# Product 1 of the next block placed between products 5 and 3 in stages 2 and 4

## The chip, the cores and the metric

The kernel runs on one core of a Trainium2 chip. The metric is device time in microseconds (us), the median of repeated runs. Five instruction streams matter: TensorE (PE in the profile; its weight loads have a column of their own, PEld), VectorE (DVE), ScalarE (ACT), GpSimd (POOL) and SyncE (SP), whose queue issues all the transfers (DMA) between HBM and the on-chip memory.

## The reference

Three layers are chained. An attention with 32 memory slots per head is computed for 8 batches of 576 tokens and 8 heads of width 64:

```python
a = exp(phi - max(phi)); a = a / (sum(a) + 1e-9)
k_m, v_m = a^T k, a^T v                      # 32 x 64 per head
attn = softmax(q k_m^T / 8);  x = attn v_m   # 4608 x 512 after joining heads
```

Two feed-forward layers follow, on 4608 tokens with model width 512 and inner width 2048:

```python
h = x @ w_in;   g = s * relu(h)**2 + b;          x = g @ w_out
h = x @ w2_in;  g = h / (1 + exp(-1.702 * h));   y = g @ w2_out
```

## The kernel before, in words

All operands are float32. A product of two float32 matrices is made of three matmuls, since each operand is split into a high part (the cast to the matmul's format, `hi`, on ACT or DVE) and the rest (`lo`, a subtraction on DVE): high by high, high by low, low by high.

The work has four stages. Stage 1 makes, for every batch, the attention and the first inner product `h` with its `relu`, and sends the result `r` to HBM. Stage 2 (`down` with the name "wo") reads `r`, squares it on ACT and multiplies with `w_out`; stage 3 (`up`) makes the second inner product and its gate; stage 4 (`down` with the name "w2") makes the last product. Stages 2 to 4 go through 8 blocks of 576 tokens. In each block the product is made by Strassen's scheme in Winograd's form: seven products of half-size matrices instead of eight. They are numbered 1 to 7. In stages 2 and 4 each product runs over four quarters q of the inner dimension, and one quarter is a group of 12 matmuls of 288 columns (L611 to L613 of the profile): a product has 48 matmuls, a block 336, a stage 2688.

The seven products of a block go into three accumulators, tiles of PSUM: X (products 1, 6, 5 and 3, added one upon the other), Z (product 2) and Y (products 7 and 4). Since X goes on being added to, it has to be read out between products: after product 1 into `a`, after product 6 into `u2`, after product 5 into `u4`, after product 3 into the result `c12` (`leave`, L619; the copies are on ACT, L637 in stage 2 as two halves of 288 columns, L631 in stage 4 as one of 576). The group that adds to X next must wait for that copy. All accumulators, the `h` of stage 1 and some small products share one ring of 4 PSUM tiles ("ps" in `BUFS`, L179). The operands of the products, their quarters A, B, C, D, E and most results share a ring of 38 tiles ("t"), the weights a ring of 32 ("w"); of those, seven hold the kept quarter 3 of `w_out` and 21 more its other quarters throughout stage 2.

Nothing in this is put in order by hand. Every operation is given to `Order.add` with a due time, the engines that may do it, and what it reads and writes; `Order.sort` (L65) then plays the whole program with a cost for each operation and at each step takes, among the operations that could start soonest on an engine, those with the earliest due time. What comes out is the order of instructions on each engine, and each engine works through its own in order. A tile of a ring is given out in the order of due times too. In `down` the due time of quarter q of product i is `due + pos[i] * pas + q * step`, where `pas` is a seventh of a block (6.4) and `pos` (L576) the product's place. The loads of its operands are due 14 to 16 ahead of that (L583), their squares 5 ahead, the differences of quarters 4 ahead, the high and low parts 2.5 ahead.

Of the kernel before, what the change touches and what calls it, by code (L numbers as in the profile page):

```python
# [152 lines left out]
class Net:  # L153
# [415 lines left out]
    def down(self, name, src, s, due, prior, first):  # L569

        nc, T, HS = self.nc, self.T, self.HS
        pas = self.B2 / 7
        step = pas / 4
        X, Y, Z = (("ps", (x, name, s)) for x in "XYZ")
        G = [[("t", (x, name, s, q)) for x in "ABCDE"] for q in range(4)]
        pos = {1: 0, 2: 1, 6: 2, 7: 3, 5: 4, 3: 5, 4: 6}  # L576
        to = {1: X, 2: Z, 6: X, 7: Y, 5: X, 3: X, 4: Y}
        n = 2 * HS
        for x, i in zip((0, 2, 1, 3), (1, 2, 6, 6)):
            for q in range(4):  # L580
                d = due + pos[i] * pas + q * step
                k = G[q][x]
                self.load(d - 14 - 2 * (x == 1), k, src, s, q, x // 2, x % 2)  # L583
                if name == "wo":
                    self.on_act(d - 5, n, lambda k=k: nc.scalar.activation(T[k], T[k], AF.Square), (), (k,))
        for i, at in pos.items():
            for q in range(4):
                A, Bk, C, D, E = G[q]
                d = due + at * pas + q * step
                x = {1: A, 2: C, 6: E, 7: Bk, 5: A, 3: D, 4: C}[i]  # L590
                if i == 6:
                    self.minus(d - 4, A, Bk, A)
                    self.minus(d - 3.5, E, D, A, new=True)
                elif i == 7:
                    self.minus(d - 4, Bk, D, Bk)
                elif i == 4:
                    self.minus(d - 4, C, C, E)
                h, l = self.operand(d - 2.5, i, (name, s, q), x, n)
                w = ("w", (name, i, q) if (name, i, q) in self.kept else (name, i, q, 1))

                def mm(i=i, q=q, h=h, l=l, w=w):
                    z = to[i]
                    if q == 0 and i in (1, 2, 7):
                        self.pst(z)
                    for o in range(2):
                        out = T[z][:, o, 0:HS]
                        for p in range(2):
                            c = slice(256 * p + 128 * o, 256 * p + 128 * o + 128)
                            f = q == p == 0 and i in (1, 2, 7)
                            last = q == 3 and p == 1  # L610
                            nc.tensor.matmul(out, T[w][:, 0, c], T[h][:, p], start=f, stop=False, skip_group_check=True)  # L611
                            nc.tensor.matmul(out, T[w][:, 0, c], T[l][:, p], start=False, stop=False, skip_group_check=True)  # L612
                            nc.tensor.matmul(out, T[w][:, 1, c], T[h][:, p], start=False, stop=last, skip_group_check=True)  # L613

                self.pe(d, 12 * HS, mm, (h, l, (*w, "h"), (*w, "l")), (to[i],))
            d = due + (at + 1) * pas
            self.leave(name, s, i, to[i], d, X, Y, Z)
# [154 lines left out]
    def plan(self):  # L772
        B, B1, B2 = self.B, self.B1, self.B2
        t2 = B * B1
        self.order.until = t2
        t3, t4 = t2 + B * B2, t2 + 2 * B * B2
        self.kept = {("wo", i, 3) for i in range(1, 8)}
        self.warm(True)
        for i, x in enumerate(("moe_s", "moe_b")):
            self.dma(10, lambda i=i: self.sc[:, i:i + 1], lambda x=x: self.a[x].partition_broadcast(P), (), (("sc", 0, i),), 1)  # L780
        for b in range(B):
            s0 = b * B1
            if b == 0:
                for g in range(2):
                    self.slots(0, g, -42 + 4 * g, 10)
                    self.attend(0, g, -28 + 4 * g)
                self.warm(False)
            for j in range(4):
                if b == 0:
                    for c in range(4):  # L790
                        k = ("w", ("wi", j, c // 2))

                        def make(k=k, c=c):
                            if c % 2 == 0:
                                self.t(k, [P, 2, 512])
                            return self.T[k][:, c % 2]

                        self.convert(9.6 * j - 24 + 2 * c, (*k, c % 2), make, self.a["wi"][4 * j + c], 24 - 2 * c if j == 0 else 6)
                d = s0 + j * B1 / 4
                self.matrix(b, j, d - 8)  # L800
                for i in range(2):
                    for u in range(2):
                        self.step(b, 2 * j + i, u, d + B1 / 16 * (2 * i + u))
                if b + 1 < B and j < 2:
                    self.slots(b + 1, j, s0 + 2 + 8 * j)
                elif b + 1 < B:
                    self.attend(b + 1, j - 2, s0 + 18 + 7 * (j - 2))
            if b in (2, 3, 4, 6):
                q = (2, 3, 4, 6).index(b)
                self.prepare("wo", q, s0 + 2, keep=q == 3, step=3)  # L810
        for q in range(3):
            for i in range(1, 8):
                self.weights("wo", i, q, t2 - 12 + 6.2 * (1, 2, 6, 7, 5, 3, 4).index(i) + q * 1.5)
        for s in range(B):
            self.down("wo", "r", s, t2 + s * B2, None, s == 0)
        for q in range(4):
            self.prepare("w1", q, t2 + 10 + 115 * q, step=4)
        for q in range(4):
            for at, i in enumerate((1, 2, 6, 7, 5, 3, 4)):
                self.weights("w1", i, q, t3 - 14 + 11 * q + 1.5 * at)  # L820
        for s in range(B):
            self.up(s, t3 + s * B2)
        for q in range(4):
            self.prepare("w2", q, t3 + 10 + 65 * q, step=4)
        for at, i in enumerate((1, 2, 6, 7, 5, 3, 4)):
            for q in range(4):
                self.weights("w2", i, q, t4 - 14 + 6.2 * at + 1.5 * q)
        for s in range(B):
            self.down("w2", "g", s, t4 + s * B2, None, s == 0)
# [76 lines left out]
```

## Time and profile before

| | |
|---|---|
| median of 3 runs | 1437.73 us (1436.1 to 1439.28) |
| profiled execution, its own time | 1438.46 us |
| its span, first to last instruction | 1436.4 us |
| PE matmuls busy | 1400.5 us, 98% of the span |
| DVE, ACT busy | 1098.2 us (76%), 762.4 us (53%) |
| DMA | 329.19 MB, mean 229 GB/s |

The profile is one execution, and the span is 2.06 us shorter than the time of that execution. A matmul is shown with a length of about 0.29 us, while the next one starts about 0.13 us after it, because they are pipelined; so an idle time that the profile shows in front of a matmul is shorter than what the stream of matmuls loses there.

### The profile page before, as it was taken

What the parts mean: (1) busy time and instruction counts of PE and PEld (TensorE: products, weight loads), DVE (VectorE), ACT (ScalarE), POOL (GpSimd) and SP (SyncE); (2) the same over time, 40 slices, a digit from 0 to 9 for tenths busy, and PEclk for the clock granted to TensorE, in tenths of its full rate; (3) what the DMA queues carried; (4) which work ended last, traced back from release to release, by engine and by line L of the source; (5) the groups of instructions that cost most, each with busy time, mean ns of one, the idle gap of its engine ahead of it and who ended that gap; (6) DMA issues with size and microseconds to landing.
All of it is one profiled execution on the core that took longest, in us unless ns stands there. A gap on an engine that the chain in (4) does not pass through costs nothing.

```text
span 1436.4 us, 28622 instructions
## 1 busy us (share of the span) xinstructions
PE 1400.5 (98%) x11190; PEld 1340.0 (93%) x11190; DVE 1098.2 (76%) x1728; ACT 762.4 (53%) x1224; POOL 94.7 (7%) x70
## 2 busy tenths in 40 slices
PE   6899999999999999999999999999999999999998
PEld 5778877789999999999999999999999999999998
DVE  7879998986898988898895565752458787777872
ACT  4455654566676666665565555554444434243441
POOL 1400110100101000100110010100000000000000
PEclk9899999999999999999999999999999999999999
DMA  9979999899954465475998756473598433554330
GB/s 354 322 258 340 353 322 344 289 309 366 313 181 131 140 238 149 156 256 171 346 347 318 278 180 239 169 266 133 188 357 310 127 116 108 156 157 131 114 104 34
DMA packets 136775, 329.19 MB, mean 229 GB/s; under 512 B 15552, under 2 KB 15552, under 8 KB 136640
## 3 DMA queue, kind: packets, MB, share of 16 engines
q1 hardware_dynamic: 136640, 327.37, 66.2%
q8 instruction: 88, 1.44, 0.4%
q14 instruction: 47, 0.39, 0.1%
HBM read 192.56 MB, written 134.74 MB: 228 GB/s over the span
## 4 chain that ended last, share of the span: by engine, by line
PE 50%; DMA 1%; DVE 0%; issue 0%; ACT 0%; SPq 0%; DVEq 0%
PE X L611 5%; PE X L613 5%; PE X L612 5%; PE X L718 5%; PE X L720 5%; PE X L719 5%; PE Y L611 3%; PE Y L613 3%; PE Y L612 3%; PE Y L718 2%; PE Y L720 2%; PE Y L719 2%; PE Z L611 1%; PE Z L613 1%; PE Z L612 1%; PE Z L718 1%
## 5 line engine op out<-in xcount | busy, mean ns | idle before, releaser
L263 PE MATMUL h<-ah,mh 128*128 128x288 f32 x512 | 160.5, 313 | 4.7 <-DVE ah L242 4.5
L265 PE MATMUL h<-ah,ml 128*128 128x288 f32 x512 | 154.3, 301 | 9.3 <-DVE ml L247 9.1
L611 PE MATMUL X<-oh,wo 128*128 128x288 f32 x512 | 152.7, 298 | 9.8 <-ACT u L637 9.7
L264 PE MATMUL h<-al,mh 128*128 128x288 f32 x512 | 154.2, 301 | 2.1 <-DVE al L247 2.1
L611 PE MATMUL X<-oh,w 128*128 128x288 f32 x512 | 151.7, 296 | 0.7 <-ACT u L631 0.7
L718 PE MATMUL X<-oh,w 128*128 128x288 f32 x512 | 151.7, 296 | 0.2 <-DMA w<-w 0.2
L612 PE MATMUL X<-ol,wo 128*128 128x288 f32 x512 | 151.6, 296 | 0.0
L719 PE MATMUL X<-ol,w 128*128 128x288 f32 x512 | 151.1, 295 | 0.3 <-DVE ol L247 0.3
L612 PE MATMUL X<-ol,w 128*128 128x288 f32 x512 | 151.0, 295 | 0.0
L613 PE MATMUL X<-oh,wo 128*128 128x288 f32 x512 | 151.0, 295 | 0.0
L720 PE MATMUL X<-oh,w 128*128 128x288 f32 x512 | 150.5, 294 | 0.0
L613 PE MATMUL X<-oh,w 128*128 128x288 f32 x512 | 150.5, 294 | 0.0
L247 DVE TENSOR_TENSOR h<-Y,u 128x576 f32<-128x576 f32 x64 | 48.4, 757 | 128.7 <-ACT u L726 89.5
L547 ACT ACTIVATE r<-h 128x576 f32<-128x576 f32 x122 | 79.5, 651 | 110.2 <-PE h L265 90.8
L263 PEld LDWEIGHTS h<-ah,mh 128*128 128x128 f32 x512 | 99.8, 195 | 26.7 <-ACT r L547 12.0
L247 DVE TENSOR_TENSOR ol<-C,oh 128x576 fp32r<-128x576 f32 x128 | 94.9, 753 | 21.5 <-ACT oh L241 11.4
L265 PEld LDWEIGHTS h<-ah,ml 128*128 128x128 f32 x512 | 99.2, 194 | 10.5 <-DVE ml L247 10.5
L241 ACT CAST oh<-A 128x576 fp32r<-128x576 f32 x106 | 68.1, 672 | 74.3 <-PE Y L613 29.8
L611 PEld LDWEIGHTS X<-oh,wo 128*128 128x128 f32 x512 | 96.2, 188 | 11.7 <-ACT u L637 11.7
L247 DVE TENSOR_TENSOR ol<-A,oh 128x576 fp32r<-128x576 f32 x128 | 94.7, 760 | 15.3 <-PE X L613 5.7
L264 PEld LDWEIGHTS h<-al,mh 128*128 128x128 f32 x512 | 99.2, 194 | 2.9 <-DVE al L247 2.9
L746 ACT ACTIVATE g<-h 128x576 f32<-128x576 f32 x96 | 65.8, 686 | 67.5 <-DVE h L247 64.4
(181 smaller groups left out, 4226.8 us busy)
## 6 DMA issues: line engine op xcount, KB each, us to landing
w<-w SPq DMA_DIRECT2D x112, 512.0 KB, 5.7
r<-r SPq DMA_DIRECT2D x128, 288.0 KB, 4.1
g<-g SPq DMA_DIRECT2D x128, 288.0 KB, 2.7
wo<-wo SPq DMA_DIRECT2D x42, 512.0 KB, 5.2
kv<-in_kv SPq DMA_DIRECT2D x64, 258.0 KB, 4.8
raw<-in_w SPq DMA_DIRECT2D x32, 512.0 KB, 6.1
q<-in_q SPq DMA_DIRECT2D x32, 288.0 KB, 4.9
A<-r SPq DMA_DIRECT2D x32, 288.0 KB, 3.2
```

The lines of the kernel that those rows point to most:

```text
L241: self.order.add(due, [self.act(n, lambda: nc.scalar.copy(out(), src()), psum), self.dve(n, lambda: nc.vector.tensor_copy(out(), src()), f ...
L247: self.order.add(due, [self.dve(n, lambda: nc.vector.tensor_tensor(out(), a(), b(), op=op), port=port)], r, w, first)
L263: self.nc.tensor.matmul(ps, wh, xh, start=start and i == 0, stop=False)
L264: self.nc.tensor.matmul(ps, wh, xl, start=False, stop=False)
L265: self.nc.tensor.matmul(ps, wl, xh, start=False, stop=(i == n - 1))
L547: self.act(2 * HS, lambda: nc.scalar.activation(self.two(r), T[h][:, :, 0:HS], AF.Relu), psum=True),
L611: nc.tensor.matmul(out, T[w][:, 0, c], T[h][:, p], start=f, stop=False, skip_group_check=True)
L612: nc.tensor.matmul(out, T[w][:, 0, c], T[l][:, p], start=False, stop=False, skip_group_check=True)
L613: nc.tensor.matmul(out, T[w][:, 1, c], T[h][:, p], start=False, stop=last, skip_group_check=True)
L718: nc.tensor.matmul(out, T[w][:, 0, c], T[h][:, k], start=f, stop=False, skip_group_check=True)
L719: nc.tensor.matmul(out, T[w][:, 0, c], T[l][:, k], start=False, stop=False, skip_group_check=True)
L720: nc.tensor.matmul(out, T[w][:, 1, c], T[h][:, k], start=False, stop=k == 1, skip_group_check=True)
```

## The change

`pos` gives product 1 the place -3 instead of 0 and moves products 2, 6, 7 and 5 forward by one place each; 3 and 4 stay. Three places before a block begins is place 4 of the block before it, which is left empty there: the due times of product 1 of the next block fall between those of products 5 and 3. Since the loads, squares and parts of product 1 take their due times from it, they move with it, and so does the copy `a`. For the first block of stage 2 product 1 becomes due while stage 1 is still at work. The loads of `w_out` for stage 2 are due 12 earlier (and 6.4 instead of 6.2 apart); those of stage 4 are not touched. An empty line shifts the lines below by one, so L611 to L613 are L612 to L614 after the change.

```diff
--- before.py
+++ after.py
@@ -573,7 +573,8 @@
         step = pas / 4
         X, Y, Z = (("ps", (x, name, s)) for x in "XYZ")
         G = [[("t", (x, name, s, q)) for x in "ABCDE"] for q in range(4)]
-        pos = {1: 0, 2: 1, 6: 2, 7: 3, 5: 4, 3: 5, 4: 6}
+
+        pos = {1: -3, 2: 0, 6: 1, 7: 2, 5: 3, 3: 5, 4: 6}
         to = {1: X, 2: Z, 6: X, 7: Y, 5: X, 3: X, 4: Y}
         n = 2 * HS
         for x, i in zip((0, 2, 1, 3), (1, 2, 6, 6)):
@@ -810,7 +811,7 @@
                 self.prepare("wo", q, s0 + 2, keep=q == 3, step=3)
         for q in range(3):
             for i in range(1, 8):
-                self.weights("wo", i, q, t2 - 12 + 6.2 * (1, 2, 6, 7, 5, 3, 4).index(i) + q * 1.5)
+                self.weights("wo", i, q, t2 - 24 + 6.4 * (1, 2, 6, 7, 5, 3, 4).index(i) + q * 1.5)
         for s in range(B):
             self.down("wo", "r", s, t2 + s * B2, None, s == 0)
         for q in range(4):
```

The order that comes out differs on all engines from the end of stage 1 on. Two places on TensorE follow. The names are tiles with the number of their allocation; X is the accumulator, oh and ol are the high and low parts of an operand, wo is a tile of weights.

The first place is the end of product 5 and the start of product 3 of block 5 (the sixth) in stage 2. Before, on TensorE:

```order
L611 MATMUL X_1330_7345<-oh_1382_7720,wo_739_3886 128x288
L612 MATMUL X_1330_7345<-ol_1397_7821,wo_739_3886 128x288
L613 MATMUL X_1330_7345<-oh_1382_7720,wo_739_3886 128x288
L611 MATMUL X_1330_7345<-oh_1385_7739,wo_901_4781 128x288
L612 MATMUL X_1330_7345<-ol_1401_7843,wo_901_4781 128x288
L613 MATMUL X_1330_7345<-oh_1385_7739,wo_901_4781 128x288
```

Product 3 follows upon product 5 with nothing in between, both on the accumulator X of the same block. After, on TensorE at the same place:

```order
L614 MATMUL X_1328_7350<-oh_1387_7744,wo_740_3888 128x288
L612 MATMUL X_1408_7884<-oh_1394_7785,wo_736_3867 128x288
...
L614 MATMUL X_1408_7884<-oh_1394_7785,wo_736_3867 128x288
L612 MATMUL X_1408_7884<-oh_1397_7804,wo_658_3468 128x288
...
L614 MATMUL X_1408_7884<-oh_1397_7804,wo_658_3468 128x288
L612 MATMUL X_1328_7350<-oh_1400_7825,wo_882_4655 128x288
```

Two groups of 12 matmuls, quarters 2 and 3 of product 1 of the next block, which go into another X, now stand between the last group of product 5 and the first of product 3.

The same count for every seam in stage 2 at which X is read out before it is added to again: before, no group stands between products 5 and 3 in blocks 0, 2 and 5, nor between products 6 and 5 in blocks 2 and 6; one stands between 5 and 3 in blocks 1 and 7 (and between 1 and 6 in blocks 0 and 1), and two or more at all others. After, one group stands between 5 and 3 in block 7, which has no next block, and two or more at every other seam. In stage 4 one group or more stands there both before and after, except between 5 and 3 of block 7, where none does in either.

The second place is the end of stage 1. Before, on TensorE, the last `h` of stage 1 and the first product of stage 2:

```order
L263 MATMUL h_869_4593<-ah_800_4216,mh_849_4483 128x288
L264 MATMUL h_869_4593<-al_801_4218,mh_849_4483 128x288
L265 MATMUL h_869_4593<-ah_800_4216,ml_853_4505 128x288
L611 MATMUL X_873_4614<-oh_802_4220,wo_723_3815 128x288
L612 MATMUL X_873_4614<-ol_809_4244,wo_723_3815 128x288
L613 MATMUL X_873_4614<-oh_802_4220,wo_723_3815 128x288
```

Stage 2 begins when the last group of stage 1 is through. After, on TensorE:

```order
L614 MATMUL X_847_4456<-oh_781_4104,wo_736_3867 128x288
L263 MATMUL h_866_4558<-ah_782_4106,mh_836_4390 128x288
...
L265 MATMUL h_866_4558<-ah_804_4224,ml_838_4407 128x288
L612 MATMUL X_847_4456<-oh_785_4121,wo_658_3468 128x288
...
L614 MATMUL X_847_4456<-oh_785_4121,wo_658_3468 128x288
L263 MATMUL h_872_4597<-ah_782_4106,mh_836_4390 128x288
```

The quarters of product 1 of block 0 (X) now stand between groups of `h`: seven groups of `h` come while this X holds one of the four PSUM tiles.

## Rows read from the trace of the kernel before

**Rows 1.** The page, busy time of each engine.
```profile
PE 1400.5 (98%) x11190; PEld 1340.0 (93%) x11190; DVE 1098.2 (76%) x1728; ACT 762.4 (53%) x1224; POOL 94.7 (7%) x70
```
**Rows 2.** Busy time by stretch, stages 2 to 4; PEclk and DMA follow POOL.
```profile
345.00:710.00 365.00, 354.82 (x2634) 352.53 (x2633) 315.42 (x481) 245.13 (x413) 25.42 (x14) 1.00 0.64 213
710.00:1070.00 360.00, 359.83 (x2699) 359.60 (x2698) 211.54 (x335) 187.33 (x297) 25.47 (x18) 1.00 0.68 247
1070.00:1437.00 367.00, 361.64 (x2711) 361.17 (x2709) 275.97 (x402) 139.96 (x219) 0.00 (x0) 1.00 0.44 139
```
**Rows 3.** What PE waited for: us in total, times, longest us.
```profile
PE X L611 <- ACT u L637: 9.7, 6, 2.6
PE X L611 <- ACT u L631: 0.7, 1, 0.7
PE X L718 <- DMA w<-w: 0.2, 1, 0.2
```
**Rows 4.** Timeline of PE at seams with no group between: start, us, idle before.
```profile
373.56 0.29 PE L613 MATMUL X<-oh,wo 128*128 128x288 f32 x1
375.01 0.40 PE L611 MATMUL X<-oh,wo 128*128 128x288 f32 x1 [1.17 <-ACT u L637]
...
460.74 0.40 PE L611 MATMUL X<-oh,wo 128*128 128x288 f32 x1 [1.74 <-ACT u L637]
...
472.00 0.40 PE L611 MATMUL X<-oh,wo 128*128 128x288 f32 x1 [1.39 <-ACT u L637]
...
606.05 0.40 PE L611 MATMUL X<-oh,wo 128*128 128x288 f32 x1 [2.60 <-ACT u L637]
...
648.24 0.40 PE L611 MATMUL X<-oh,wo 128*128 128x288 f32 x1 [2.02 <-ACT u L637]
```
**Rows 5.** Timeline of PE at other seams, the last in stage 4.
```profile
366.86 0.29 PE L613 MATMUL Y<-oh,wo 128*128 128x288 f32 x1
367.19 0.40 PE L611 MATMUL X<-oh,wo 128*128 128x288 f32 x1
...
421.58 0.29 PE L613 MATMUL X<-oh,wo 128*128 128x288 f32 x1
421.94 0.40 PE L611 MATMUL X<-oh,wo 128*128 128x288 f32 x1
...
705.91 0.40 PE L611 MATMUL X<-oh,wo 128*128 128x288 f32 x1 [0.83 <-ACT u L637]
...
1419.31 0.40 PE L611 MATMUL X<-oh,w 128*128 128x288 f32 x1 [0.73 <-ACT u L631]
```
**Rows 6.** Timeline of ACT ahead of the stall that ends at 606.05.
```profile
603.21 0.68 ACT L585 ACTIVATE B<-B 128x576 f32<-128x576 f32 x1 [1.90 <-DMA B<-r]
603.80 0.66 ACT L241 CAST oh<-A 128x576 fp32r<-128x576 f32 x1
604.36 0.68 ACT L585 ACTIVATE C<-C 128x576 f32<-128x576 f32 x1
604.95 1.05 ACT L637 ACTIVATE u<-X,bw,sc 128x288 f32<-128x288 f32 x2
```
**Rows 7.** What SP's queue and ACT waited for in most of stage 2.
```profile
SPq L236 <- PE X L613: 57.8, 43, 4.4
...
ACT D L585 <- DMA D<-r: 7.3, 8, 2.5
```
**Rows 8.** The page, the evacuation of h in stage 1.
```profile
L547 ACT ACTIVATE r<-h 128x576 f32<-128x576 f32 x122 | 79.5, 651 | 110.2 <-PE h L265 90.8
```
**Rows 9.** The chain of waits: start, us, what; end of stage 2, start of stage 3.
```profile
695.36 0.15 PE Y L613
695.50 0.02 issue
695.52 8.66 DMA raw<-in_w
...
743.37 8.20 DMA w<-w
...
751.64 4.24 DMA w<-w
...
755.92 0.40 PE X L718
```

## The prediction

> **What bounds the kernel now.** I read the page first. TensorE is busy for 98% of the span, DVE for 76% and ACT for 53% [rows 1]: TensorE sets the time, and only what lets its stream of matmuls stand still can be won back. The same by stretch shows where it stands still [rows 2]. From 710 to 1070 us, nearly all of it stage 3, 359.83 of 360.00 us are busy; the window from 345 to 710, stage 2, has 354.82 of 365.00, so about 10 us are idle there; stage 4 has 361.64 of 367.00 in a window that runs past the last matmul. The granted clock reads 1.00 in all three, the upper of its two levels, 2.4 GHz. The waits of TensorE name the reason in stage 2: the first matmul of a group that adds to X waits for ACT's copy u of that X, 6 times, 9.7 us in total, 2.6 at most, and in stage 4 once, 0.7 us [rows 3].
>
> The timeline gives each of them. In stage 3 a matmul comes every 360.00/2699 = 0.133 us [rows 2]. At the end of block 0 the last matmul of product 5 starts at 373.56 and the first of product 3 at 375.01, 1.45 us later instead of 0.133: 1.32 us are lost, where the profile shows 1.17 idle [rows 4]. The rest, 0.16 us, is the overlap: 0.29 us shown for a matmul less the step of 0.133. So each idle time shown counts 0.16 more. The five stalls where no group stands between the read-out of X and the next addition to it then cost 1.33, 1.90, 1.55, 2.76 and 2.18, together 9.7 us (8.92 shown plus 5 x 0.16) [rows 4].
>
> Where one group, 12 x 0.133 = 1.6 us of work, stands between, it is less: 421.94 - 421.58 - 0.133 = 0.23 at block 1's seam, 0.83 + 0.16 = 1.0 at block 7's, and in stage 4 nothing is shown at any such seam [rows 3, 5]. One seam with two groups, at 367.19, has 367.19 - 366.86 - 0.133 = 0.20 [rows 5]. The last block of stage 4 has no group between and loses 0.73 + 0.16 = 0.9 [rows 5].
>
> Why they differ is seen on ACT. The copy itself takes 1.05 us as two halves [rows 6], and 1.32 is about what the seam costs when ACT is free. Ahead of 606.05 ACT sat idle for 1.90 us for a load of B and then did three other things before the copy started at 604.95 [rows 6]: it works in its own order, and a late load ahead of the copy is paid by TensorE at the seam, 2.76 - 1.32 = 1.4 us extra.
>
> **The change part by part.** *Seams of stage 2.* After, two or more groups stand at every seam but block 7's, that is 2 x 1.6 = 3.2 us of TensorE's work against 1.32 for the copy when ACT is free and 2.76 for the worst seen [rows 4]. So I count the five zero-group stalls as gone, 9.7 us, and the 0.23 of block 1. Block 7 keeps one group and its 1.0, and I let the 0.20 at 367.19 stay, as two groups stand there in both. The same number of matmuls runs, so nothing else changes on TensorE: -9.9 us. From both sides: nothing of this won would be 0; the most is all losses of X there, 9.9 + 1.0 + 0.2 = 11.1.
>
> The Trainium skill, "Perfetto Trace Analysis", section Identifying the Most-Contended Engine, says that matmul busy time is a poor measure of TensorE's headroom, and LDWEIGHTS busy share the better one. By that, PEld's 352.53 of 365.00 [rows 2] leaves 12.5 us, and the most that stage 2 could give would be 12.5 instead of 11.1; I stay with the start-to-start sum, which names its stalls.
>
> *Stage 4.* The seams that were covered by one group are so after, and block 7's has none in either: 0, between -0.9 (its one stall) and +0.9 (one more such).
>
> *End of stage 1.* Four groups of product 1 are moved between groups of h; the matmuls are the same. This X now holds one of four PSUM tiles while seven groups of h run through the other three. Evacuating an h takes 0.65 us [rows 8] against 1.6 for the next group, so I take 0, the cover being the very groups of product 1 that now stand between. If each of the seven had to wait out its evacuation it would be 7 x 0.65 = +4.6. The saving side is 0, since the same groups run.
>
> *Loads.* The operands A of the next block are squared, split and loaded 19 us earlier in due time, with the 4 loads, 4 squares and 8 parts of each block; in number nothing is added on SP, ACT or DVE. SP works in order: a load that waits for a free tile keeps all behind it back, the loads of B, C and D among them. In stage 2 SP did wait for tiles that TensorE frees, 43 times and 57.8 us in all, and ACT waited for D 8 times, 7.3 us, 2.5 at most [rows 7]; none of it reached TensorE by way of the operands there. I take 0; the bound above is a rival below. The weights of stage 2 are asked for earlier; no wait for them is shown in stage 2 in the waits of TensorE [rows 3]: 0.
>
> *Start of stage 3.* The chain of waits shows a second path close behind TensorE: a load of raw weights at 695.52 takes 8.66 us, and at 743.37 a write of prepared weights, 8.20, is followed by its read back, 4.24, which ends at TensorE's matmul of 755.92 [rows 9], where 0.17 us idle are left, 0.2 in the waits [rows 3]. If this path did not come earlier by as much as TensorE, the gain would be given back there. But its load at 695.52 was itself released by a matmul of stage 2 at 695.36 [rows 9], so it comes earlier with TensorE: 0, at worst +9.9.
>
> *Sum.* 1438.46 (the profiled execution: span 1436.4 and 2.06 around it) - 9.9 = 1428.5. The median of the runs, 1437.73, is 0.73 below that execution, so 1427.8 for a median; I write 1428, a gain of 0.7%. This kernel's measurements can tell 0.2%, 2.9 us, from no change.
>
> **The rivals.** *More is won.* Block 7's 1.0, the 0.2 and the stall of 0.9 in stage 4 vanish too: 2.1 more, 1425.7. Against it: the order puts no more work at these two seams of block 7 than before. Chance 0.07.
>
> *Part of it comes back.* Each of the seven seams where a next block exists keeps what one-group seams cost before, the mean of 0.23 and 1.0 [rows 5], since ACT may be later than now: 7 x 0.6 = +4.3, 1432. The exposed evacuations of h, +4.6, give nearly the same time. For it: ACT's copies wait behind late loads [rows 6]; against it: 3.2 us of cover. Chance 0.14.
>
> *The gain is given back at the start of stage 3*, or the stalls only move to other seams: the path by the raw weights keeps its time, TensorE waits at the first block of stage 3 for as long as it was earlier, 9.9 us. That is 1437.7, no change. For it: 0.17 us of idle says that this path was already late. Against it: its load is released by TensorE. Chance 0.06.
>
> *Slower: the operands starve.* Product 1's tiles are held about three products longer of the 38 in the ring, so SP's queue stands at a load without a free tile and those of B, C and D behind it land late. Place: products 6 and 7 of each block of stage 2; price: the longest wait of ACT for D, 2.5 us [rows 7], once for TensorE in each of 7 blocks, +17.5, against -9.9: 1438.5 + 7.6, some 1445 as a median. It decides from (9.9 + 2.9)/7 = 1.8 us in each block on. For it: 57.8 us of SP's waits for tiles [rows 7], and DVE is busy 315 of 365 us [rows 2]. Against it: today's stalls are put down to the copy of X, not to an operand [rows 3], and the loads have more than ten us of lead in their due times. Chance 0.05. The same page of the Trainium skill, section Optimization Strategy, says that a gap which repeats on the engine that should be saturated can mean too few buffers for the next tile; by that rule, holding tiles longer would be this rival. The trace does not bear it out: the idle ends with an ACT copy of the very X that is written next.
>
> **How the numbers follow.** The forecast, 1426.5 to 1430, has 0.68; more 0.07; part 0.14; given back 0.06; slower 0.05. Faster by over 0.2%: 0.68 + 0.07 + 0.14 = 0.89. Within: 0.06. Slower: 0.05. The range takes in the case with more and the one with part of the gain, 1425 to 1433, the upper end being 1427.8 with the bound of 4.6 for h and some tenths; it leaves out a little over one in ten.
>
> **What would show it.** In the profile after: TensorE's waits for u L637 (L638 then) fall from 9.7 us and 6 times to one of about 0.8 near the end of stage 2; stage 2 from its first Z group to its last matmul has hardly an idle time; u L631 (L632) stays at one of 0.7; DMA w in stage 3 stays below 1 us; and no wait of h appears at the end of stage 1. It would be wrong if the waits for u remained at several seams, if waits for ol or oh in X, Y or Z came up in stage 2, or if the start of stage 3 showed a wait for w of several us.

## The result and the profile after

The changed kernel takes 1424.59 us in the median (1423.55 to 1427.92), the kernel before 1437.65 beside it: a ratio of 0.9913, 95% interval 0.9893 to 0.9933. The gain is 13.1 us of medians, where 9.9 were forecast. The profiled execution took 1423.55 us with a span of 1421.6, which is 14.8 less than the span of before. Two executions of the experiments below, one of 3452.26 us and one of 1682.45 us, were slow ones and are in none of the medians and ratios.

Busy time by stretch, with the columns of [rows 2]: PE, PEld, DVE, ACT and POOL busy, the granted clock, the share and rate of the DMA.

```profile
345.00:710.00 365.00, 364.65 (x2736) 364.42 (x2735) 328.15 (x506) 252.41 (x424) 28.85 (x19) 1.00 0.67 222
710.00:1060.00 350.00, 350.00 (x2628) 350.00 (x2627) 200.31 (x317) 179.18 (x284) 18.65 (x13) 1.00 0.68 246
1070.00:1422.00 352.00, 346.81 (x2600) 346.34 (x2598) 270.18 (x402) 123.31 (x191) 0.00 (x0) 1.00 0.43 129
```

In the window from 345 to 710 TensorE now has 0.35 us of idle time instead of 10.2, and 102 more matmuls go through it in the same 365 us (2736 for 2634). DVE is busier there than before, 328 us for 315, and does not hold TensorE up.

What TensorE waited for, as in [rows 3] (us in total, times, longest):

```profile
PE X L612 <- ACT u L632: 0.7, 1, 0.7
PE X L612 <- ACT u L638: 0.3, 1, 0.3
```

These two are all that is left on X, Y and Z. The wait of 9.7 us is one of 0.3, and the wait for a weight at the start of stage 3 is gone. In the timeline of PE they are the seams between products 5 and 3 in the last block of stage 2 and of stage 4, where no next block exists (start, us, the idle time before):

```profile
691.49 0.40 PE L612 MATMUL X<-oh,wo 128*128 128x288 f32 x1 [0.35 <-ACT u L638]
...
1404.48 0.40 PE L612 MATMUL X<-oh,w 128*128 128x288 f32 x1 [0.73 <-ACT u L632]
```

The chain of waits at the end of stage 2 is as in [rows 9], some 14 us earlier: a matmul releases the load of raw weights, the load lands 8.20 us later, and what ACT does with it stands ahead of the copy u.

```profile
681.41 0.15 PE X L614
681.56 0.02 issue
681.58 8.20 DMA raw<-in_w
...
690.38 1.07 ACT u L638 x2
```

SP and ACT wait in stage 2, in the columns of [rows 7], for about as long in all as before, partly on other things:

```profile
SPq L236 <- PE X L614: 53.7, 43, 2.9
SPq L236 <- PE Y L614: 42.0, 17, 11.9
...
ACT C L586 <- DMA C<-r: 15.2, 19, 2.1
```

The loads of C have become ACT's longest wait, 19 times and 15.2 us. With two groups at every seam but block 7's, TensorE feels none of it but the 0.3 us there.

**Where the 14.8 us went.** I took from the timeline, for every matmul of stages 2 to 4, its start less the start of the one before it, and counted what is over 0.133 us. Before, this sums to 15.7 us, after to 1.7, so 14.0 of the 14.8 us are there, 13.6 of them in stage 2. The rest, 0.8, lies in stage 1, and nothing says that it is the work of the change: the 3000th matmul starts at 325.48 before and 324.67 after, TensorE's order is the same up to there, and a second profile of the changed kernel has it at 326.62. The 14.0 are:

| lost before and not after | us |
|---|---|
| five seams without a group (the term of the forecast) | 9.7 |
| block 1's seam, and 0.20 at 367.19 | 0.4 |
| block 7's seam: 1.0 before, 0.5 after | 0.5 |
| matmuls at half speed after 606.55 | 1.5 |
| the second matmul after a stall, 0.11 each, 11 before and 3 after | 0.9 |
| three small waits: 0.21 at 420 and 0.49 at 688.96 for a low part from DVE, 0.33 at 755.92 for a weight | 1.0 |

The last line is not shown to be the work of the change: a second profile of the changed kernel has 0.8 us more of such small losses than the first, 2.5 for 1.7. The fourth line had not been seen in the profile of before. This is its timeline on PE just after its longest stall, from the second matmul on (the first is at 606.05, [rows 4]):

```profile
606.29 0.29 PE L612 MATMUL X<-ol,wo 128*128 128x288 f32 x1
606.42 0.29 PE L613 MATMUL X<-oh,wo 128*128 128x288 f32 x1
606.55 0.37 PE L611 MATMUL X<-oh,wo 128*128 128x288 f32 x1
606.72 0.44 PE L612 MATMUL X<-ol,wo 128*128 128x288 f32 x1
606.96 0.44 PE L613 MATMUL X<-oh,wo 128*128 128x288 f32 x1
607.20 0.44 PE L611 MATMUL X<-oh,wo 128*128 128x288 f32 x1
```

Half a microsecond after the stream starts again, a matmul takes 0.44 us instead of 0.29 and the next starts 0.24 after it instead of 0.13; this goes on until 610.06. In the granted clock (after the busy times) it is seen when the stretch is cut short, here the 6 us after that stall and, for comparison, after the one of 2.02 us at 648.24:

```profile
606.00:612.00 6.00, 5.95 (x33) 5.95 (x34) 4.80 (x7) 2.73 (x5) 0.00 (x0) 0.72 0.60 178
648.20:654.20 6.00, 5.96 (x44) 5.96 (x45) 5.59 (x10) 4.33 (x7) 0.00 (x0) 1.00 0.63 197
```

TensorE is busy for the whole of both; at a mean clock of 0.72 it gets 33 matmuls through and at 1.00 it gets 44. The half-speed matmuls ran at the lower level, 1.2 GHz. In the window of 365 us in [rows 2] the same clock is rounded to 1.00. The 1.5 us are those of this one execution; how many falls there are in another is not known, and stage 4 alone, whose stage 2 is in the order of before, shows its one fall at another stall (below).

### The profile page after: what moved, and what is told of

It is laid out like the page before. It is cut to its first block, busy times and chain, and to the rows that moved or that the text cites. A ratio compares the mean times of both kernels' runs of the same rounds, so it can differ in the third digit from the quotient of the medians.

```text
span 1421.6 us, 28599 instructions
## 1 busy us (share of the span) xinstructions
PE 1396.8 (98%) x11190; PEld 1338.2 (94%) x11190; DVE 1105.3 (78%) x1750; ACT 751.0 (53%) x1202; POOL 91.4 (6%) x70
## 4 chain that ended last, share of the span: by engine, by line
PE 90%; DVE 5%; DMA 4%; issue 0%; ACT 0%; SPq 0%; DVEq 0%; ACTq 0%
PE X L612 10%; PE X L614 9%; PE X L613 9%; PE X L719 5%; PE Y L612 5%; PE Y L614 5%; PE X L721 5%; PE Y L613 5%; PE X L720 5%; PE h L263 4%; PE h L265 4%; PE h L264 4%; PE Y L719 2%; PE Z L612 2%; PE Z L614 2%; PE Y L721 2%
## 5 line engine op out<-in xcount | busy, mean ns | idle before, releaser
L612 PE MATMUL X<-oh,w 128*128 128x288 f32 x512 | 151.7, 296 | 0.7 <-ACT u L632 0.7
L612 PE MATMUL X<-oh,wo 128*128 128x288 f32 x512 | 151.7, 296 | 0.3 <-ACT u L638 0.3
L613 PE MATMUL X<-ol,wo 128*128 128x288 f32 x512 | 151.0, 295 | 0.0
L613 PE MATMUL X<-ol,w 128*128 128x288 f32 x512 | 151.0, 295 | 0.0
L614 PE MATMUL X<-oh,wo 128*128 128x288 f32 x512 | 150.5, 294 | 0.0
L614 PE MATMUL X<-oh,w 128*128 128x288 f32 x512 | 150.5, 294 | 0.0
L241 ACT CAST oh<-C 128x576 fp32r<-128x576 f32 x94 | 62.3, 673 | 104.0 <-PE X L613 79.6
L612 PEld LDWEIGHTS X<-oh,wo 128*128 128x128 f32 x512 | 95.9, 187 | 1.4 <-issue 0.8
```

## The experiments

Each ran beside the kernel before on the same chip.

**Stage 2 alone.**

```diff
-        pos = {1: -3, 2: 0, 6: 1, 7: 2, 5: 3, 3: 5, 4: 6}
+        pos = {1: -3, 2: 0, 6: 1, 7: 2, 5: 3, 3: 5, 4: 6} if name == "wo" else {1: 0, 2: 1, 6: 2, 7: 3, 5: 4, 3: 5, 4: 6}
```

> The new places of the products in stage 2 alone, the old ones in stage 4. Theory A (the gain is the stalls of stage 2, where X is read out with nothing between): the whole gain, 1424 to 1426 us, TensorE's waits for u in stage 2 one of at most 1 us. Rival B (a good part comes from the re-planned order as a whole, stage 4 and the shares of DVE and ACT included): some 3 us of the 13 missing, 1427 to 1429.

1425.03 us, ratio 0.9905 (0.9889 to 0.9921): the whole gain. TensorE waits for u once in stage 4, 0.7 us, and not at all in stage 2.

**Stage 4 alone** (the kernel before, with the new places where the name is "w2").

```diff
-        pos = {1: 0, 2: 1, 6: 2, 7: 3, 5: 4, 3: 5, 4: 6}
+        pos = {1: -3, 2: 0, 6: 1, 7: 2, 5: 3, 3: 5, 4: 6} if name == "w2" else {1: 0, 2: 1, 6: 2, 7: 3, 5: 4, 3: 5, 4: 6}
```

> The new places in stage 4 alone, old places and old due times of the weights in stage 2. Theory A: no change, 1436 to 1439 us, with the stalls of stage 2 as before (9 to 10 us shown, waits for u). Rival B: about 3 us faster, 1434 to 1435.

1437.74 us, ratio 1.0000 (0.9987 to 1.0014): nothing, and TensorE's waits in stage 2 are there again:

```profile
PE X L611 <- ACT u L637: 8.9, 7, 1.8
```

So the gain is that of stage 2, as theory A has it, and rival B falls. Here too the clock fell once, after another stall than in the profile of before (the 6 us from the end of the stall of 1.74 us idle, at 461.50):

```profile
461.50:467.50 6.00, 6.00 (x33) 6.00 (x34) 2.95 (x5) 3.64 (x6) 0.09 (x1) 0.72 0.44 145
```

**The weights not asked for earlier.**

```diff
-                self.weights("wo", i, q, t2 - 24 + 6.4 * (1, 2, 6, 7, 5, 3, 4).index(i) + q * 1.5)
+                self.weights("wo", i, q, t2 - 12 + 6.2 * (1, 2, 6, 7, 5, 3, 4).index(i) + q * 1.5)
```

> The new places in both stages, the loads of w_out due as before the change. Theory A: the first load of those weights was issued some 60 us ahead of its use before, so 12 us less matter not: 1424 to 1426 us, no wait for weights at the start of stage 2. Rival C (the earlier weights are needed): a wait for wo of several us at the first products of stage 2, 1428 or more.

1424.84 us, ratio 0.9901 (0.9879 to 0.9923): this part of the change does nothing that can be measured. TensorE waits for no weight at the start of stage 2, and rival C falls.

**Product 1 between 3 and 4.**

```diff
-        pos = {1: -3, 2: 0, 6: 1, 7: 2, 5: 3, 3: 5, 4: 6}
+        pos = {1: -2, 2: 0, 6: 1, 7: 2, 5: 3, 3: 4, 4: 6}
```

> Product 1 of the next block due between products 3 and 4 instead of between 5 and 3. The built order has one or two groups at every seam of stage 2 after product 5 and none without any. Theory A (any ready work at the seam does it, and the planner draws it forward): within 2 us of the changed kernel, 1424 to 1427 us; the two seams with one group may show up to 1 us each. Rival D (the place between 5 and 3 itself is what counts): the stalls after product 5 come back, 5 or more of them at 1.3 us and more, 1431 or more.

1425.76 us, ratio 0.9909 (0.9891 to 0.9926), as the changed kernel. The place between 5 and 3 is not what counts: in the built order groups of product 1 of the next block stand between products 5 and 3 here too, so the planner itself draws them forward to the seam. One of the two seams with a single group shows in the waits:

```profile
PE X L612 <- ACT u L638: 0.6, 1, 0.6
```

**The kernel before, with each copy out of X in stage 2 done twice.**

```diff
-                    nc.scalar.activation(T[k][:, o], T[X][:, o, 0:HS], AF.Identity, bias=self.bw[:, 2 * half + o:2 * half + o + 1], scale=self.sc[:, 0:1])
+                    for _ in range(2):
+                        nc.scalar.activation(T[k][:, o], T[X][:, o, 0:HS], AF.Identity, bias=self.bw[:, 2 * half + o:2 * half + o + 1], scale=self.sc[:, 0:1])
```

> The kernel before, each copy out of X in stage 2 done twice in the same place (the order is unchanged), which makes it 1.05 us longer. Theory A with the clock (a stall costs its length, and where it is long TensorE's clock falls to 1.2 GHz for some us after it, as the trace of before shows after 606.05): the five seams without a group lose 1.05 more each, those with one group up to 1.05 each, 6 to 9 us together, and after the longest stalls rows of half-speed matmuls come, 1.5 us each: 1446 to 1454 us, and a granted clock well under 1 in the us after several seams. Rival E (the half-speed matmuls after 606.05 have nothing to do with the stall's length): 1444 to 1448, with no more such rows than before.

1455.52 us, ratio 1.0134 (1.0117 to 1.0151), 18.5 us more than before and 1.5 above the range that was expected. By the same count as above TensorE loses 32.6 us in stages 2 to 4, 16.9 more. The waits:

```profile
PE X L611 <- ACT u L638: 19.0, 9, 3.5
PE X L611 <- ACT a L638: 1.6, 2, 0.8
```

9.3 us more of waiting on u and 1.6 on a are what longer copies cost. Of the rest, 5.4 us are 50 more matmuls at half speed. The clock in the 6 us from each of its six longest stalls on (they end with 2.41, 3.03, 2.50, 3.43, 3.49 and 1.89 us idle):

```profile
376.70:382.70 6.00, 5.96 (x33) 5.96 (x34) 5.98 (x10) 6.00 (x11) 0.00 (x0) 0.72 0.67 191
467.30:473.30 6.00, 5.98 (x45) 5.99 (x46) 3.91 (x7) 3.49 (x6) 0.94 (x1) 1.00 0.45 156
479.70:485.70 6.00, 6.00 (x34) 6.00 (x35) 4.17 (x7) 1.84 (x3) 0.77 (x1) 0.72 0.28 88
616.70:622.70 6.00, 6.00 (x35) 6.00 (x36) 4.81 (x8) 3.01 (x6) 0.00 (x0) 0.76 0.49 139
660.10:666.10 6.00, 6.00 (x33) 6.00 (x34) 4.72 (x7) 3.50 (x6) 0.00 (x0) 0.72 0.21 58
676.60:682.60 6.00, 6.00 (x34) 6.00 (x35) 4.28 (x7) 4.44 (x8) 0.00 (x0) 0.72 0.36 136
```

At five of the six the clock fell to the lower level, against one of five before: rival E falls, and with longer stalls there were more falls. The granted clock over the whole span says the same of the other executions: 0.986 in each of the three, against 0.990 to 0.993 in the eight of the kernel before beside them. But length alone does not say which: at the stall with 3.03 us idle there was no fall, at the one with 1.89 there was. Nor does the fall need the stream to start again first: in the stall that ends at 616.66 the clock had already fallen while TensorE stood still.

```profile
616.20:616.60 0.40, 0.00 (x0) 0.00 (x0) 0.00 (x0) 0.40 (x2) 0.00 (x0) 0.50 0.30 114
```

**The changed kernel with the same doubled copies.**

> The changed kernel with the same doubled copies. Theory A: two groups, 3.2 us, cover a copy of 2.1 us too, so only the seam of the last block pays: 1424 to 1428 us. Rival F (ACT's load in stage 2 is what TensorE waits for, now that it does 34 us more there): 1430 or more, with waits for u or for operands at several seams.

1429.0 us, ratio 0.9946 (0.9929 to 0.9963). That is 26.5 us below the kernel before with the same copies, but 4.4 above the median of the changed kernel (the intervals of the two ratios still overlap) and just over what I expected. The profiled execution is the slowest of its four, 1432.28 us. In it several seams did show, four of them with two groups between, which theory A had as covered:

```profile
PE X L612 <- ACT u L639: 4.3, 5, 1.4
```

The longest, at 562.89, on ACT (start, us, the idle time before):

```profile
559.36 0.69 ACT L586 ACTIVATE D<-D 128x576 f32<-128x576 f32 x1 [1.39 <-DMA D<-r]
559.95 1.20 ACT L639 ACTIVATE u<-X,bw,sc 128x288 f32<-128x288 f32 x2
561.05 0.67 ACT L586 ACTIVATE B<-B 128x576 f32<-128x576 f32 x1
561.63 1.21 ACT L639 ACTIVATE u<-X,bw,sc 128x288 f32<-128x288 f32 x2
```

ACT waits 1.39 us for a load of D, then does the first half twice, a square of B, and the second half twice. Two groups give 3.2 us; a copy of 2.1 us with a late load ahead of it and another operation within it goes beyond that. In the profile of the changed kernel, with the copy of 1.05 us, no seam with two groups shows a wait. So the cover is not boundless, and rival F is half right: ACT's order comes into it when the copy is twice as long.

**The same order, one place earlier.**

```diff
-        pos = {1: -3, 2: 0, 6: 1, 7: 2, 5: 3, 3: 5, 4: 6}
+        pos = {1: -1, 2: 0, 6: 1, 7: 2, 5: 3, 3: 4, 4: 5}
```

> Product 1 of the next block due right after product 4, as before the change, but every product and its loads due one place earlier. The built order has six seams of stage 2 without a group. Theory A: no gain, 1436 to 1442 us, with stalls of 1.3 us and more at those six. Rival G (what helps is that the loads and operands of a block start earlier): 1428 to 1433.

1444.6 us, ratio 1.0058 (1.0038 to 1.0079): slower than before, by more than I expected. Rival G falls. The waits:

```profile
PE X L612 <- ACT u L638: 11.4, 6, 2.9
PE X L719 <- DMA w<-w: 1.2, 1, 1.2
```

Six stalls at the six seams, two falls of the clock, and at the start of stage 3 a wait of 1.2 us for a weight, the path of [rows 9]. Its profiled execution, 1441.3 us, lies 3.3 below the median of its runs, and of that difference I have no trace.

**The last block woven.** In the last block of both stages products 2 and 7 are due later and products 6, 5, 3 and 4 earlier, so that the groups of 2 and 7 fall to the read-outs of X:

```diff
+        if s == self.B - 1:
+            pos = {1: -3, 2: 1.5, 6: 0, 7: 3, 5: 1.5, 3: 4, 4: 5}
```

> The changed kernel, and in the last block of stages 2 and 4 product 2 is due later, so that its groups and those of product 7 stand at the read-outs of X; the built order has one group or more at every seam of stage 4 as well. Theory A: the 0.9 us of stage 4's last block goes, stage 2 keeps its 0.5: 1 us faster than the changed kernel, 1423 to 1424.5 us. Rival: the stall moves to product 7 or 2, no difference.

1424.97 us, ratio 0.9918 (0.9901 to 0.9935): no faster than the changed kernel. In stage 4 the stall shrank from 0.9 to 0.27 us, in stage 2 the last block's grew from 0.5 to 1.5:

```profile
689.88 0.40 PE L614 MATMUL X<-oh,wo 128*128 128x288 f32 x1 [1.30 <-ACT u L640]
```

In the built order two groups stand at this seam, where the changed kernel has one, and the copy is the single one of 1.05 us; still TensorE waited. ACT shows why:

```profile
687.07 0.67 ACT L283 ACTIVATE cw<-raw 128x512 f32<-128x512 f32 x1 [1.95 <-DMA x<-c]
687.64 0.66 ACT L241 CAST oh<-x 128x576 fp32r<-128x576 f32 x1
688.21 0.58 ACT L640 ACTIVATE u<-X,bw,sc 128x288 f32<-128x288 f32 x1
688.69 0.65 ACT L283 ACTIVATE cw<-raw 128x512 f32<-128x512 f32 x1
689.25 0.57 ACT L640 ACTIVATE u<-X,bw,sc 128x288 f32<-128x288 f32 x1
```

It sat idle for 1.95 us until a transfer of x landed, and three other operations, one of them between the halves of the copy, came on top. So two groups cover the read-out only as long as nothing late stands ahead of it on ACT.

The new places were then tried in stage 4 alone (`if s == self.B - 1 and name == "w2":`), beside the changed kernel run once more on the same chip.

> The changed kernel with the later product 2 in the last block of stage 4 alone; stage 2 as in the changed kernel. The earlier run with both had its stall of 0.9 us in stage 4 shrunk to 0.27 and a longer one in stage 2 in exchange (1.47 for 0.51). Theory A: stage 4's stall goes and stage 2 keeps 0.5: 0.7 us faster than the changed kernel beside it, which the times alone can hardly tell; the profile shows it. Rival: the stall in stage 4 only moves, no difference in the sum of TensorE's stalls.

> The changed kernel unaltered, beside the other one on the same chip. 1424 to 1426 us; its sum of stalls after stage 1 as in the first profile, 1.7 us, if what was read there repeats.

1424.17 us (ratio 0.9899, 0.9882 to 0.9915) beside 1426.11 for the changed kernel (0.9908, 0.9890 to 0.9927): lower, but not apart by these intervals. In the traces it is plainer. TensorE loses 0.4 us in stages 2 to 4 of this version, by the count above, and 2.5 in the changed kernel run again, which had 1.7 in its first profile. The stall of 0.9 us in the last block of stage 4, which both profiles of the changed kernel have, is gone and has not moved; the rest of the difference is small waits that differ between those two profiles as well. In this version the window of stage 2 has no idle time on TensorE (the clock of 1.00 and the DMA's share at the end):

```profile
345.00:710.00 365.00, 365.00 (x2738) 364.89 (x2738) 327.71 (x504) 251.72 (x423) 27.21 (x18) 1.00 0.67 222
```

In this execution 0.4 us are left from stage 2 on for an order to win. That this version is the faster of the two is not shown by the times.

## Why the prediction came out as it did

The mechanism of the forecast was right. The stalls of stage 2 are gone at the five seams without a group, and the runs with one stage each show that the whole gain is theirs. Stage 4 gave 0, as the sum had it. The seven groups of h that share three PSUM tiles at the end of stage 1 brought no wait (from 325 to 350 us TensorE waits for nothing); the loads of operands moved earlier brought none to TensorE, though ACT waits oftener for C; and the second path at the start of stage 3 came earlier with TensorE, as its release by a matmul had said. Block 7's seam stayed, at 0.5 instead of the 1.0 kept for it, and in the second profile of the changed kernel it does not show. The doubled copies in the kernel before are the counter-proof: longer read-outs cost where nothing stands at the seam, and much less where two groups do (10.9 us of added waits for 4.0).

What was off is a size: the term "Seams of stage 2", -9.9 us, for which the traces have 12.9 (the table without its last line and without the second matmuls elsewhere), and the bound given with it, "the most is all losses of X there, 9.9 + 1.0 + 0.2 = 11.1". The stalls themselves were measured rightly, 9.7 us at the five seams. The step that failed is that the sum took a stall to end where TensorE starts again. It does not. The matmuls after it are slow, 0.11 us lost with the second one after each stall and 1.5 us where the clock falls to 1.2 GHz. The row that would have told, a clock of 0.72 in the 6 us after 606, was to be had before; I read the clock in windows of 365 us, where it is 1.00. The 0.20 at 367.19 and half of block 7's 1.0 went as well. The three small waits, 1.0 us, were in no term and in none of the rivals: the prediction saw the one for a weight and counted it as nothing to be won.

Together these put the median 3.4 us below the 1428 of the forecast, under its 1426.5 to 1430 and 0.4 below 1425, the lower end of the range that took in the rivals. That it comes so near this end is luck. The end was set by the case "More is won", for block 7's 1.0, the 0.2 and the stall of stage 4; of these 2.1 us only 0.7 came, and the matmuls after the stalls, which no case held, made up for the rest.

The Trainium skill's measure that was weighed there, the LDWEIGHTS busy share ("Perfetto Trace Analysis", Identifying the Most-Contended Engine), gave 12.5 us as the most that stage 2 could give, and 13.6 came there. It is closer than the sum of the waits, but in the 6 us after 606 the weight loads are shown as busy for 5.95 us at a clock of 0.72, so what the clock costs is not in it. The other rule, that a repeating gap can mean too few buffers (Optimization Strategy), did not hold for these gaps: after the change the tiles of product 1 are asked for earlier and so held longer, and the gaps are gone.

On the falling clock the skill says, in "TensorE: Matmul & The Clock Gate", section Loop structure matters more than you think, that a long wait for DMA between the matmuls takes the clock down and that matmuls kept back to back stay at the upper level. The traces agree in kind, though the waits here were for ACT's copy: each of the falls shown above began within a stall of TensorE or at most 1.6 us after its end, and the changed kernel, which keeps no stall over 0.9 us there, has none in stages 2 to 4. They add what the section does not speak of, that a single stall in a dense stream can be enough, and that of the two longest of the kernel before only one was (0.72 after 606, 1.00 after 648).

## What to carry to other kernels

Where an accumulator is read out and added to again, count in the built order the independent work that stands between the two, and compare it with the read-out including what may be queued ahead of it on its engine; none costs the whole read-out, one group was on the edge here, and two were enough in the changed kernel but not in the woven last block, where a late transfer held ACT up ahead of the copy, nor with a copy twice as long. Where the due time puts that work matters less than that it comes early enough: due one place later than in the change, its groups were still drawn to the seam; due two later, six seams of stage 2 were left without any. Price a stall on TensorE by the matmuls after it as well, and look at the granted clock in windows of a few us around the stall, not over a stage.

## What had not been expected of the hardware

TensorE's clock fell to its lower level at single stalls in a stream that was otherwise dense: in the profiles once in the kernel before (2.60 us idle), once with stage 4 alone (1.74 us idle), five times with doubled copies in it (1.89 to 3.49 us idle), twice with the same order one place earlier (2.67 and 1.79 us idle). Each fall cost 1.1 to 1.6 us, in 10 to 15 matmuls that came 0.24 us apart instead of 0.133. Why it falls at one stall and not at a longer one is open; no run here settles it.
